# Rebuilding the middle part of a transformer kernel: loads, engines, order of tiles, and the hand-over to the last matrix products

## The chip, the cores and the metric

One core of one Trainium2 chip. The metric is the device time of one execution in microseconds (us); a version's time is the median of several executions, and a version is compared with the kernel before within one series of runs on one chip. The profile is one execution, recorded instruction by instruction.

In profile lines PE is TensorE (PEld its weight loads), DVE is VectorE, ACT is ScalarE, POOL is GpSimd; SPq and ACTq are the DMA queues of SyncE and ScalarE; L411 is a line of that run's own kernel. A timeline line gives start, duration, engine, line, what was done and how often, and in brackets the engine's idle time before it and what ended that. A line of waits gives who waited for whom, the total in us, the number of waits and the longest. "..." stands for lines left out. A "product" is one matmul instruction.

## The reference, cut to what matters

A recurrent attention over 64 segments (part A) gives `a`. Then, on 2048 rows of 1024 columns:

```python
h  = x + A(layernorm(x), ...)                 # part A: 64 segments, one after the other
# B, applied to hn = layernorm(h):
h1 = gelu(layernorm(hn) @ w1)                 # 1024 x 1024
#   four column groups of h1 shifted by -1, +1, -2, +2 rows
x1 = hn + shifted(h1) @ w2                    # 1024 x 1024
h2 = gelu(layernorm(x1) @ w3) @ w4            # 1024 x 3584 x 1024
out = h + x1 + h2
```

I call what stands up to `x1` and its normalised transpose `zT` the middle part (w1, w2), and the products with w3 and w4 the last part.

## The kernel before

Rows come in 16 tiles of 128, four tiles to a block. The middle part works by whole blocks: stage 1 of block b+1 (four tiles of sums, two norms, transposes, then 64 products with w1), then stage 2 of block b (for each tile 16 products with w2, a norm, transposes).

```python
def ln_apply(dst, src, tag):
    mv = _ln_stats(nc, sm, src, D, tag)             # VectorE: two bn_stats, one bn_aggr
    r = _rstd(nc, sm, mv, eps_t, tag)               # GpSimd: add, pow on 128x1
    nc.vector.tensor_scalar(dst[:], src[:], mv[:, 0:1], r[:], op0=ALU.subtract, op1=ALU.mult)

with tc.tile_pool(name="b1w", bufs=1) as b1w, tc.tile_pool(name="b1", bufs=2) as b1, ...:
    nc.sync.dma_start(w1[:], ...); nc.sync.dma_start(w2[:], ...); nc.sync.dma_start(w3[:], ...)

    def stage1(b):
        for tl in range(TPB):
            nc.scalar.dma_start(xt[:], x2[...]);  nc.scalar.dma_start(at[:], a_d[...])
            nc.gpsimd.tensor_tensor(ht[:], xt[:], at[:], op=ALU.add)
            nc.scalar.dma_start(h_d[...], ht[:])
            ln_apply(hn, ht, "l1"); ln_apply(u, hn, "l2")
            # eight transposes of u into PSUM on TensorE
            nc.vector.tensor_copy(uT[:, :, tl * 128:(tl + 1) * 128], pt[:])
        # 64 products with w1, a gelu on ScalarE after every eight

    def stage2(b):
        for tl in range(TPB):
            # 2 x 8 products with w2, x1 = ps + hn on VectorE
            ln_apply(z, x1, "l3")
            # eight transposes of z into PSUM
            nc.vector.tensor_copy(zT[:, :, tl * 128:(tl + 1) * 128], pt[:])
        nc.scalar.dma_start(zT_d[b], zT[:])
    # ... (loop over blocks left out)

wb4 = ctx.enter_context(tc.tile_pool(name="wb4", bufs=1))
nc.sync.dma_start(w4[:], ...)                       # 7 MB
with tc.tile_pool(name="b2", bufs=2) as b2:
    for b in range(NB):
        zT = b2.tile([128, NC, BT], BF16, tag="zT2")
        nc.scalar.dma_start(zT[:], zT_d[b])
        # 28 x 8 products with w3 and gelu, 8 x 28 products with w4, sums, output (left out)
```

A pool is a range of on-chip memory. A pool that is opened over the place of a closed one waits, by default, for that whole pool; `reuse_waits="tile"` makes its tiles wait for just the tiles that lay there.

## Time and profile before

| | before |
|---|---|
| median time | 2928.3 us (13 runs, 2924.8 to 2935.5) |
| part A (to its last product) | 2274.6 us |
| to the first product with w1 ("head") | 50.5 us |
| first w1 product to first w3 product | 206.5 us |
| last part | 392.3 us |

The stages are read from the order of TensorE's instructions in time. The whole span in 40 slices (73 us each), with TensorE's busy tenths and its granted clock in tenths:

```profile
PE   1599999999999999999999999999999367699999
PEclk9999999999999999999999999999999688899999
```

The reader is to see that after the start a single stretch, slices 32 to 35, is not full: 257 us in which the array waits and, after its longer waits, starts again at a low clock.

### The profile page before, as it was taken

How to read it: one execution, taken by the hardware profiler on the slowest of the kernel's cores; microseconds unless marked ns; L12 is line 12 of the kernel's file. 1: busy time of each engine (PE TensorE's matmuls, PEld its weight loads, DVE VectorE, ACT ScalarE, POOL GpSimd, SP SyncE). 2: the span in 40 equal slices, each digit the busy share in tenths (PEclk: the TensorE clock that was granted, in tenths of full speed). 3: DMA queues.
4: the chain of work that ended last, by engine and by line, in shares of the span. 5: the costliest groups of instructions: out<-in, count | busy, mean ns of one | idle time of the engine just before them, and what ended most of it. 6: DMA issues, size and time to landing. Idle time of an engine off the chain costs nothing.

```text
span 2923.9 us, 69270 instructions
## 1 busy us (share of the span) xinstructions
PE 2629.8 (90%) x29824; PEld 1517.4 (52%) x29824; DVE 1015.7 (35%) x3043; ACT 739.5 (25%) x1506; POOL 286.4 (10%) x496
## 2 busy tenths in 40 slices
PE   1599999999999999999999999999999367699999
PEld 1365555655655655555656655555555133344444
DVE  3233333333343333343333343333443454300000
ACT  1122222322233322332222233222232011112211
POOL 4000000000000000000000000000000431110110
PEclk9999999999999999999999999999999688899999
DMA  9999999999999999999999999999999721511010
GB/s 355 332 352 338 330 324 334 340 333 340 328 325 332 338 336 341 327 330 335 337 338 330 331 335 338 331 339 323 332 333 325 286 91 43 210 47 39 30 44 15
DMA packets 254227, 816.15 MB, mean 279 GB/s; under 512 B 28120, under 2 KB 52696, under 8 KB 252896
## 3 DMA queue, kind: packets, MB, share of 16 engines
q1 hardware_dynamic: 232256, 761.36, 72.7%
q0 software_dynamic: 11296, 25.20, 2.7%
q10 hardware_dynamic: 10368, 25.17, 2.3%
q8 instruction: 233, 3.82, 0.5%
q14 instruction: 74, 0.61, 0.1%
HBM read 775.44 MB, written 36.18 MB: 278 GB/s over the span
## 4 chain that ended last, share of the span: by engine, by line
PE 80%; DMA 9%; DVE 4%; POOL 3%; issue 2%; ACT 1%; SPq 0%; ACTq 0%; POOLq 0%
PE ps L207 41%; PE Uacc L290 15%; PE ps L454 7%; PE ps L469 7%; PE pr L215 6%; DMA a_d<-usb 4%; DMA xt<-in_A_x_dram 2%; PE ps L411 2%; PE pv L274 1%; DVE st L28 1%; PE ps L239 1%; POOL ht L397 1%; DVE usb L297 1%; ACT usb L296 1%; DMA at<-a_d 1%
## 5 line engine op out<-in xcount | busy, mean ns | idle before, releaser
L207 PEld LDWEIGHTS <-hT 128*64 128x64 bf16 x12288 | 723.6, 110 | 504.9 <-issue 55.0
L207 PE MATMUL ps<-ringw,hT 128*64 128x512 bf16 x3840 | 795.6, 380 | 10.7 <-DMA ringw<-in_A_Wk_dram 5.2
L210 ACT CAST Tsb<-ps 128x512 bf16<-128x512 f32 x768 | 447.5, 585 | 1029.0 <-PE ps L207 772.3
L207 PE MATMUL ps<-wq,hT 128*64 128x512 bf16 x3072 | 488.4, 382 | 25.9 <-DVE hT L302 24.0
L207 PE MATMUL ps<-wv,hT 128*64 128x512 bf16 x3072 | 486.7, 380 | 0.7 <-ACT Tsb L210 0.7
L290 PE MATMUL Uacc<-wo,oT 128*40 128x512 bf16 x2560 | 345.6, 381 | 0.5 <-ACT oT L277 0.5
L207 PE MATMUL ps<-wk,hT 128*64 128x512 bf16 x2304 | 322.5, 380 | 0.0
L290 PEld LDWEIGHTS <-oT 128*40 128x40 bf16 x4096 | 218.2, 100 | 179.7 <-issue 8.6
L226 DVE COPY QT<-pr 128x320 bf16<-128x320 bf16 x256 | 83.1, 324 | 514.1 <-PE pr L215 512.1
L290 PE MATMUL Uacc<-ringw,oT 128*40 128x512 bf16 x1536 | 234.0, 380 | 5.4 <-DMA ringw<-in_A_Wo_dram 4.5
L454 PE MATMUL ps<-zT,w 128*128 128x512 bf16 x896 | 195.5, 381 | 17.6 <-DMA zT<-zT_d 17.6
L469 PE MATMUL ps<-w,h3T 128*128 128x512 bf16 x896 | 194.0, 379 | 0.0
L215 PEld LDWEIGHTS <-Tsb 128*64 128x64 bf16 x4096 | 153.7, 110 | 71.3 <-ACT Tsb L210 22.9
L215 PE MATMUL pr<-ident,Tsb 128*64 128x128 bf16 x4096 | 171.2, 220 | 17.3 <-ACT Tsb L210 16.9
L242 DVE SCALAR_TENSOR_TENSOR ps<-ps,maskb 128x160 f32<-128x160 f32 x256 | 85.0, 332 | 276.3 <-PE ps L239 274.3
L315 POOL COPY hT<-xt 128x256 bf16<-128x256 bf16 x64 | 25.6, 400 | 1535.2 <-PE ps L207 1532.7
L254 DVE TENSOR_TENSOR Pp<-ps,sm 64x160 bf16<-64x160 f32 x512 | 165.1, 322 | 16.7
L277 ACT CAST oT<-pv 128x320 bf16<-128x320 f32 x256 | 110.2, 430 | 224.6 <-PE pv L274 220.5
L471 DVE TENSOR_TENSOR ot<-ps,rs 128x512 bf16<-128x512 f32 x32 | 22.1, 691 | 383.9 <-PE ps L469 383.9
L454 PEld LDWEIGHTS <-w 128*128 128x128 bf16 x896 | 87.9, 98 | 124.4 <-DMA zT<-zT_d 17.8
L264 DVE COPY pt<-pr 128x512 bf16<-128x512 bf16 x256 | 107.2, 419 | 128.6 <-PE pr L215 128.5
L456 ACT ACTIVATE h3T<-ps 128x512 bf16<-128x512 f32 x112 | 66.9, 597 | 329.5 <-PE ps L454 329.5
(74 smaller groups left out, 1867.8 us busy)
## 6 DMA issues: line engine op xcount, KB each, us to landing
ringw<-wst_d SPq DMA_DIRECT2D x1323, 512.0 KB, 5.9
w<-in_B_w_dram SPq DMA_DIRECT2D x2, 7168.0 KB, 29.3
wst_d<-ringw SPq DMA_DIRECT2D x21, 512.0 KB, 4.1
wq<-in_A_Wq_dram SPq DMA_DIRECT2D x12, 512.0 KB, 11.1
wv<-in_A_Wv_dram SPq DMA_DIRECT2D x12, 512.0 KB, 12.0
wo<-in_A_Wo_dram SPq DMA_DIRECT2D x10, 512.0 KB, 13.2
wk<-in_A_Wk_dram SPq DMA_DIRECT2D x9, 512.0 KB, 10.9
xt<-in_A_x_dram POOLq DMA_DIRECT2D x16, 256.0 KB, 6.1
```

The lines of the kernel that those rows point to most:

```text
L207: nc.tensor.matmul(ps[64 * j:64 * j + 64, :], lhsT=hT[:, c, :], rhs=ws[j][:, c4, :], start=(c == 0), stop=(c == NC - 1), tile_position=(0, ...
L210: nc.scalar.copy(sb[:], ps[:])
L215: nc.tensor.transpose(dst[64 * eh:64 * eh + 64, :], src[:, 64 * eh:64 * eh + 64], ident[:], tile_position=(0, 64 * eh))
L226: nc.vector.tensor_copy(dst[:, :, 0:R].rearrange("p (j hh) r -> p hh j r", j=2), pr[:].rearrange("p hh (j r) -> p hh j r", j=2)[:, :, :, 0:R],
L242: nc.vector.scalar_tensor_tensor(sc[:], ps[:], scale, maskb[:, None, :].to_broadcast([128, 4, R]), op0=ALU.mult, op1=ALU.add)
L254: nc.vector.tensor_tensor(pp[64 * j:64 * j + 64, :, 64 * j:64 * j + R], ex[64 * j:64 * j + 64], sm[64 * j:64 * j + 64, :, None].to_broadca ...
L264: nc.vector.tensor_copy(pt[:], pr[:])
L277: nc.scalar.copy(o[:].rearrange("p (j hh) q -> p hh j q", j=2), pv[:])
L290: nc.tensor.matmul(U[64 * dr:64 * dr + R, :], lhsT=o[:, lh, :], rhs=w[:, h2, 512 * dr:512 * dr + 512], start=(first and h4 == 0), stop=(la ...
L454: nc.tensor.matmul(ps[:], lhsT=w3[:, c, fb * 128:(fb + 1) * 128], rhs=zT[:, c, :], start=(c == 0), stop=(c == NC - 1))
L456: nc.scalar.activation(h3T[:, fb, :], ps[:], ACTF.Gelu_apprx_tanh)
L469: nc.tensor.matmul(ps[:], lhsT=h3T[:, fb, tl * 128:(tl + 1) * 128], rhs=w4[:, fb, dr * 512:(dr + 1) * 512], start=(fb == 0), stop=(fb == N ...
```

## The change

Its intent: fill the middle part's gaps. Inputs are loaded ahead of the weights and w3 later; the normalisations and one copy go from VectorE to ScalarE, the sum from GpSimd to VectorE, the second norm's statistics are worked out from the first's; the blocks are interleaved tile by tile; the last part's buffers are split and wait per tile, w4 comes in quarters.

```diff
     def ln_apply(dst, src, tag):
         ...
-        nc.vector.tensor_scalar(dst[:], src[:], mv[:, 0:1], r[:], op0=ALU.subtract, op1=ALU.mult)
+        nb_ = sm.tile([128, 1], F32, tag=tag + "_nb")
+        nc.vector.scalar_tensor_tensor(nb_[:], mv[:, 0:1], -1.0, r[:], op0=ALU.mult, op1=ALU.mult)
+        nc.scalar.activation(dst[:], src[:], ACTF.Identity, bias=nb_[:], scale=r[:])
...
+    def load_xa(tt):                       # xt and at, four buffers each
+        nc.sync.dma_start(xt[:], x2[tt * 128:(tt + 1) * 128, :])
+        li = nc.sync.dma_start(at[:], a_d[tt * 128:(tt + 1) * 128, :])
+    for tt0 in range(4):
+        first_ld = load_xa(tt0)
+    with tc.issue_after(first_ld.ins):
         nc.sync.dma_start(w1[:], ...)
         nc.sync.dma_start(w2[:], ...)
-        nc.sync.dma_start(w3[:], ...)
...
+        nc.vector.tensor_tensor(ht[:], xt[:], at[:], op=ALU.add)      # was GpSimd
+        nc.gpsimd.dma_start(h_d[tt * 128:(tt + 1) * 128, :], ht[:])   # was ScalarE's queue
+        mv, r = ln_apply(hn, ht, "l1")
+        nc.gpsimd.tensor_tensor(r2[:], r[:], r[:], op=ALU.mult)
+        nc.gpsimd.tensor_scalar(r2[:], r2[:], mv[:, 1:2], LN_EPS, op0=ALU.mult, op1=ALU.add)
+        nc.gpsimd.tensor_tensor(r2[:], r2[:], eps_t[:], op=ALU.pow)
+        nc.scalar.activation(u[:], hn[:], ACTF.Identity, scale=r2[:])
...
-        for b in range(NB):
-            stage1(b)
-            if b > 0:
-                stage2(b - 1)
-        stage2(NB - 1)
+    for b in range(NB + 1):
+        for tl in range(TPB):
+            if b + 1 < NB:
+                s1_tile(b + 1, tl)
+            if b < NB:
+                m1_part(b, range(tl * npart, (tl + 1) * npart))
+            if b > 0:
+                m2_tile(b - 1, tl)         # copies zT with nc.scalar.copy
+    with tc.issue_after(last_ld[0].ins):
+        for q in range(4):                 # w3 in quarters, after the last input
+            nc.sync.dma_start(w3[...], w3v[...])
...
-    wb4 = ctx.enter_context(tc.tile_pool(name="wb4", bufs=1))
-    nc.sync.dma_start(w4[:], ...)
-    with tc.tile_pool(name="b2", bufs=2) as b2:
-            zT = b2.tile([128, NC, BT], BF16, tag="zT2")
-            nc.scalar.dma_start(zT[:], zT_d[b])
+    b2z = ctx.enter_context(tc.tile_pool(name="b2z", bufs=2, reuse_waits="tile"))
+    wb4 = ctx.enter_context(tc.tile_pool(name="wb4", bufs=1, reuse_waits="tile"))
+    for q in range(4):
+        nc.sync.dma_start(w4[...], w4v[...])
+    with tc.tile_pool(name="b2", bufs=2, reuse_waits="tile") as b2:
+            zT = b2z.tile([128, NC, BT], BF16, tag="zT2")
+            nc.sync.dma_start(zT[:], zT_d[b])
```

(Cut: shapes, buffer counts, the other stores moved from ScalarE's to GpSimd's queue, the last part's loads moved to the SP queue with one `rs` buffer instead of two.)

## The prediction

> **What bounds the kernel now.** I read the busy slices of the page first, then the table of stretches, then the waits of TensorE, then the chain of waits in order of time, and last the groups of instructions for durations. In the slices TensorE is at 9 tenths from the second slice to slice 31, drops for eight slices and is full again: the program is a long recurrent part, a middle part with gaps, and two large matrix products. The diff touches only what comes after the recurrence, so I cut the span at the last recurrent tail (2274.6 us), the first product with w1 (2325), the last transposes of z (2514) and the first product with w3 (2531.5).
>
> The table of stretches (length, busy time of TensorE, its weight loads, VectorE, ScalarE, GpSimd, then granted clock, DMA share, GB/s):
> ```profile
> 0.00:2274.60 2274.60, 2098.89 (x27264) 1271.80 (x27264) 861.71 (x2754) 652.24 (x1360) 163.00 (x334) 1.00 0.94 334
> 2274.60:2325.00 50.40, 4.12 (x32) 3.19 (x33) 21.74 (x46) 0.37 (x1) 21.95 (x27) 0.54 0.92 345
> 2325.00:2514.00 189.00, 138.47 (x736) 66.78 (x735) 109.44 (x213) 20.07 (x33) 50.17 (x88) 0.86 0.22 80
> 2514.00:2531.50 17.50, 0.00 (x0) 0.00 (x0) 0.66 (x1) 0.00 (x0) 2.23 (x4) 0.50 1.04 406
> 2531.50:2923.90 392.40, 388.38 (x1792) 175.60 (x1792) 22.12 (x32) 66.86 (x112) 49.04 (x44) 1.00 0.13 45
> ```
> The first and last rows are full of matrix work at full clock. The three between are 257 us, in which TensorE is busy 143 us, part of it at a low clock (0.54, 0.86, 0.50). ScalarE is nearly empty there (20 us), VectorE has 132 us. That is the only place where the change can win.
>
> Who makes TensorE wait in 2274.6 to 2531.6:
> ```profile
> PE pt L406 <- DVE u L372: 68.2, 11, 22.4
> PE pt L433 <- DVE z L372: 24.1, 16, 5.7
> PE ps L454 <- DMA zT<-zT_d: 17.6, 1, 17.6
> PE ps L411 <- DVE uT L407: 4.4, 4, 1.9
> ```
> It waits for normalised tiles (u, z) from VectorE, 92 us, and once for a reload of zT. The chain of waits just before that reload and the last rows of it:
> ```profile
> 2512.70 0.56 DVE z L372
> 2513.31 0.64 PE pt L433 x8
> 2513.97 0.70 DVE zT L434
> 2514.69 7.78 DMA zT_d<-zT
> 2522.56 8.94 DMA zT<-zT_d
> 2531.55 8.51 PE ps L454 x32
> ```
> The reload is of block 0, written long before; it stands behind the store of block 3 because the new pool waits for the whole old pool, and both transfers run beside the 7 MB load of w4. Pure waiting, 17.6 us.
>
> The head, in order of time:
> ```profile
> 2276.76 0.67 ACTq L395 DMA_DIRECT2D at<-a_d  x1
> 2284.29 2.11 POOL L397 TENSOR_TENSOR ht<-xt,at 128x1024 bf16<-128x1024 bf16 x1 [7.52 <-DMA w<-in_B_w_dram]
> ...
> 2309.77 2.12 POOL L397 TENSOR_TENSOR ht<-xt,at 128x1024 bf16<-128x1024 bf16 x1 [7.86 <-DMA at<-a_d]
> ...
> 2325.06 16.23 PE L411 MATMUL ps<-uT,w 128*128 128x512 bf16 x64 [1.94 <-DVE uT L407]
> ```
> The first tile's input waits behind w1 and w2; w3 (7 MB, issued at 2293) then delays the next tiles, and the first add on GpSimd takes 2.11 us. Four tiles need 50 us.
>
> Durations used below, from the groups of the same stretch:
> ```profile
> L397 POOL TENSOR_TENSOR ht<-xt,at 128x1024 bf16<-128x1024 bf16 x16 | 33.9, 2117 | 76.7 <-DVE hn L372 53.3 <-DMA at<-a_d 15.9 <-DMA w<-in_B_w_dram 7.5
> L37 POOL TENSOR_TENSOR r<-r,eps_t 128x1 f32<-128x1 f32 x48 | 27.7, 580 | 3.2
> L28 DVE BATCH_NORM_STATS2 st<-x 128x6 f32<-128x512 bf16 x32 | 21.9, 685 | 0.4
> L427 DVE TENSOR_TENSOR x<-ps,hn 128x512 bf16<-128x512 f32 x32 | 21.7, 678 | 52.8 <-PE ps L425 52.7
> L413 ACT ACTIVATE h1T<-ps 128x512 bf16<-128x512 f32 x32 | 18.8, 597 | 125.8 <-PE ps L411 121.9 <-POOL r L37 3.5 <-issue 0.4
> ```
>
> **What the Trainium skill says.** (1) "TensorE: Matmul & The Clock Gate", "Wait — 56ns, not 53.3ns?": 512 columns take 215.7 ns warm and 426.7 cold, and part 1 that some 3.4 us of idling brings the cold state. The trace agrees: eight products per gelu, gelus 1.727 us apart, 0.216 each; and after each long gap weight loads 0.43 us apart and a granted clock of 0.5. (2) "ScalarE: Activation LUTs", "What ACT_TABLE_LOAD costs" and "Table sets": 186 ns plus 0.833 per element, about 93 more for each per-partition pointer, and copy and identity lie in every table set. The trace has 1012 ns for a 1024-element copy (186 + 853 = 1039) and 597 for a 512-element gelu (613), and one table load of 1.28 us in this part; no run has identity beside gelu yet. (3) "VectorE: DVE Perf Modes", the perf-mode tier table: a two-input add of bf16 in SBUF runs at 2 elements a cycle; my estimate from that page's formula is (512 + 151)/0.96 = 0.69 us for 1024. The trace has no such instruction. (4) "DMA: Bandwidth & Descriptors", "Queues, rings and completion order": issuing queues share the same 16 engines, each engine round-robins between them and takes each queue in ring order. The 7.5 us wait of the first tile, on another queue than w1 and w2, agrees.
>
> **The change, part by part.**
>
> VectorE per tile, before: six bn_stats 4.05, three aggregations 0.6, three normalisations 1.74 (0.54 + 0.65 + 0.55), two transposed copies 1.36, two adds from PSUM 1.36: 9.1 us, times 16 = 146. After: the statistics of hn are gone (the second norm's variance is worked out from the first's), and the normalisations and one copy go to ScalarE; added are the sum 0.69 and two one-element products, about 0.19 each as an aggregation (0.20): 4 x 0.68 + 2 x 0.2 + 0.38 + 0.69 + 0.68 + 1.36 = 6.2 us.
> ScalarE per tile, after: hn and z about 186 + 853 + 2 x 93 = 1.22 each, u 1.13, zT copy 1.01, two gelus 1.2: 5.8 us, less about 0.09 of overlap each, 5.2 to 5.8.
> GpSimd per tile: out goes the 2.12 us add and one of three rstd pairs (0.22 + 0.58); in come about 1.0 for r2 and two store issues of about 0.57: 2.12 + 2.4 = 4.5 before, about 3.8 after.
> TensorE per tile: 32 products x 0.216 = 6.9, two times eight transposes about 0.45 warm: 7.8. So TensorE becomes the bound of this part, if the order lets it.
>
> The head: inputs of four tiles (2 MB) go ahead of w1 and w2, w3 comes only after the last input. Landing at about +3.5 us (a late, undisturbed input took 2.9 to 3.0), then VectorE 3.0 us per tile (0.69 + 1.36 + 0.2 + 0.19 + 0.68) for four tiles, 12, and the last tile's latency (rstd 1.1, hn 1.2, u 1.1, transposes 1.0 cold, copy 0.7) about 5: 20 us instead of 50.4. **Saves 30.**
> The body is interleaved tile by tile. First block, w1 products alone: four tiles of 16 x 0.216 + 0.45 + 0.6 for waits = 4.5, plus 1.7 for the cold start: 20. Twelve full tiles at 7.8 + 0.5 for waits: 100. Last block, w2 products alone: now every tile took 4.52 us (z transposes at 2486.45 and 2490.97); z is 0.65 slower on ScalarE and has one small step more, but zT leaves VectorE's loop: 4.7 x 4 = 19. Sum 139 instead of 189. **Saves 50.**
> The transition: waits per tile instead of per pool, with zT's buffers where w1 lay and w3 long there. zT of block 0 can arrive during the last block, so the w3 products follow at once; the z transposes of the last tile slip in among them. w4 (7 MB, 33.6 us to landing) must wait for h1T, but has 224 x 0.216 = 48 us before its first use. **Saves 17.5**, and the cold start of 1.7 is not paid again.
> The last 392 us: the loads on another queue, one rs buffer instead of two. The sum (2.11 us) must follow the previous tile's last eviction (0.69) and has 28 x 0.216 = 6 us until it is needed: 0.
>
> Sum: 2927 - 30 - 50 - 17.5 - 1.7 = 2828 us.
>
> **Rivals.** A: *the zT reload queues behind w4.* Both are now on one queue, w4 first in the program. If the order in the queue is the program's, zT waits for the last use of h1T and then shares with 7 MB: some 20 to 25 us of stall, 2850. Against it: zT is ready to issue an iteration earlier and the order follows readiness. I give it one in four.
> B: *a new chain.* With z on ScalarE, behind gelus and other copies in strict order, and a fixed order on TensorE, tiles could take 10 us instead of 8.3: 12 x 1.7 = +20, 2848. For it: VectorE was already at only 109 of 189 us, so latency and not load made the waits. Against it: stage 1 now runs a whole block ahead, so u is ready long before.
> C: *table switches.* If identity needed its own set, each tile would pay at least four switches of 1.28, 82 us or more, ScalarE at 11 us per tile becomes the bound, and the gain shrinks to some 50 us: 2875. The skill's table sets speak against it.
> D: *the head is bound by bandwidth*: 4 MB before w1 is whole, at 345 GB/s 12 us; below 20, so hidden.
>
> **Range and chances.** Time **2828 us**; A and B each cost some 20, both together give the upper end, a smooth order with tiles at 7.8 and a head of 16 us the lower: **2806 to 2858**. Faster by over 2% means below 2868.5, 58 of the 99 us expected; the head and the transition alone give 47. Chances: faster 0.94, within 2% 0.05, slower 0.01.
>
> **What would show it.** The first w1 product about 20 us after the last tail; the first w3 product about 159 us after it, with no wait for zT; VectorE about 100 us and ScalarE about 90 in that stretch; one table load; a granted clock near 1 from the first block on; the last stretch still 390 to 392. Wrong would be: tiles over 10 us with TensorE waiting for ScalarE; a gap of 20 us before the w3 products; a changed recurrent part; a stop of TensorE at the first w4 product.

## The result, and the profile after

The changed kernel took 2839.9 us (8 runs, 2835.8 to 2844.8) against 2928.3 us. The ratio is 0.9698, 95% interval 0.9688 to 0.9707. A ratio here is the mean time of one kernel's fast runs over that of the other's fast runs of the same rounds, so it is not quite the ratio of the medians quoted.

The table of stretches of the changed kernel, cut at part A's last product, the first w1 product, the start of the second block, the end of its last full tile, and the first w3 product (columns as in the prediction):

```profile
0.00:2276.90 2276.90, 2100.98 (x27264) 1272.65 (x27264) 861.37 (x2754) 651.92 (x1360) 163.01 (x334) 1.00 0.93 333
2276.90:2301.40 24.50, 4.17 (x34) 3.19 (x33) 11.75 (x25) 10.77 (x10) 10.96 (x26) 0.58 0.95 345
2301.40:2323.20 21.80, 17.98 (x97) 8.23 (x97) 15.30 (x34) 15.21 (x18) 13.42 (x31) 0.92 0.69 240
2323.20:2424.20 101.00, 95.03 (x539) 44.69 (x539) 55.13 (x109) 52.44 (x61) 33.31 (x76) 1.00 0.45 169
2424.20:2446.90 22.70, 16.80 (x104) 8.21 (x103) 13.73 (x28) 10.25 (x9) 7.63 (x16) 0.95 0.47 168
2446.90:2839.90 393.00, 389.27 (x1794) 175.84 (x1792) 22.12 (x32) 67.88 (x113) 34.56 (x17) 0.99 0.16 57
```

From the end of part A to the first w3 product it was 257 us and is 170. Its main row, 101 us, has TensorE busy 95 at full clock. VectorE fell from 132 to 96 us in this part, ScalarE rose from 20 to 89. The last part did not gain. Who makes TensorE wait in the middle part now:

```profile
PE pt L430 <- ACT u L427: 21.3, 4, 12.7
PE pt L461 <- ACT z L374: 11.9, 16, 4.3
PE ps L438 <- DVE uT L431: 2.8, 2, 2.0
```

92 us of waiting for normalised tiles became 33, of which 19.5 are the head's two waits (12.69 and 6.85). The 17.6 us wait for zT has no line any more. What is left is in four places. The timeline of the changed kernel shows each: in the head (2287), at the first block's end (2323), once in every tile (2343 and 2352), and at the end of the middle part (2446):

```profile
2287.50 0.69 DVE L417 TENSOR_TENSOR ht<-xt,at 128x1024 bf16<-128x1024 bf16 x1 [0.24 <-DMA h_d<-ht]
...
2323.18 1.67 PE L438 MATMUL ps<-uT,w 128*128 128x512 bf16 x7 [2.00 <-DVE uT L431]
...
2343.55 0.62 PE L461 MATMUL pt<-ident,z 128*128 128x128 bf16 x8 [0.53 <-ACT z L374]
...
2352.22 0.62 PE L461 MATMUL pt<-ident,z 128*128 128x128 bf16 x8 [0.53 <-ACT z L374]
...
2446.07 1.03 PE L461 MATMUL pt<-ident,z 128*128 128x128 bf16 x8 [4.25 <-ACT z L374]
2446.89 23.44 PE L497 MATMUL ps<-zT,w 128*128 128x512 bf16 x97
```

The two steady tiles give the period: 2352.22 - 2343.55 = 8.67 us.

One caution for all comparisons below: part A, which no edit touches, ended between 2270 and 2279 us in the profiles, a scatter larger than the smallest effects. I therefore give for each run both its time and, from its profile, the three stages after part A (head; first w1 to first w3 product; last part). Before: 50.5, 206.5, 392.3, together 649.3 us. Changed: 24.5, 145.5, 393.0, together 563.0 us.

### The profile page after: what moved, and what is told of

Same layout as the page of the kernel before. It is cut to its first block, busy times and chain, and to the rows that moved or that the text cites. A ratio compares the mean times of both kernels' runs of the same rounds, so it can differ in the third digit from the quotient of the medians.

```text
span 2839.9 us, 69387 instructions
## 1 busy us (share of the span) xinstructions
PE 2624.2 (92%) x29824; PEld 1512.8 (53%) x29824; DVE 979.4 (34%) x2979; ACT 808.5 (28%) x1570; POOL 262.9 (9%) x500
## 4 chain that ended last, share of the span: by engine, by line
PE 82%; DMA 9%; DVE 3%; ACT 2%; issue 2%; POOL 1%; SPq 0%; ACTq 0%; POOLq 0%; DVEq 0%
PE ps L207 42%; PE Uacc L290 14%; PE ps L497 7%; PE ps L512 7%; PE pr L215 6%; DMA a_d<-usb 4%; DMA xt<-in_A_x_dram 2%; PE ps L453 2%; DMA ringw<-wst_d 2%; PE pv L274 1%; PE ps L239 1%; DVE usb L297 1%; ACT usb L296 1%; DVE st L28 1%; ACT z L374 1%
```

## The experiments

Twelve kernels ran; all gave correct results. The kernel before took 2925.7 us in the first series (e1 to e4), 2924.9 in the second (e6, e7, e8, e10) and 2929.8 in the third (e5, e11, e12, e13), which ran on another chip than the first two. Runs of different series, the changed kernel's own among them, are therefore compared by their ratios to the kernel before and by stages. The edits are cut to the lines that matter, and some are put in words.

### Each part alone

**e1_transition.** The kernel before with only the hand-over changed:

```diff
+    b2z = ...tile_pool(name="b2z", bufs=2, reuse_waits="tile")
-    wb4, b2: default waits; w4 in one load; zT from pool b2, loaded from ScalarE's queue
+    wb4, b2: reuse_waits="tile"; w4 in quarters; zT from pool b2z, loaded from SP's queue
```

> The kernel before with the transition alone changed: zT, w4 and the second part's pools wait per tile, w4 in quarters, zT loaded from the SP queue. My theory: the 17.6 us wait for zT before the first w3 product vanishes, all else as before: 2928 - 17.5 = 2910 us. The changed kernel showed no gain beyond that there (its last stretch was 393.0 us against 392.4), so no extra cold start is expected to be saved. Rival A (zT queues behind w4 on SP): w4's first quarters must wait for h1T, zT lands late, 2920 us or no gain.

Measured: 2908.6 us, ratio 0.9943 (0.9927 to 0.9960), 17.0 us faster by the medians. Stages 50.3, 191.2, 392.4. The amount is as expected and the last part shows no further gain. Rival A did not come: zT went out at 2481.88, w4 at 2509.39. Which of the edit's four pieces did it, this run can't tell.

**e2_head.** The kernel before with only the loads changed:

```diff
-        w1, w2, w3 first on SP; xt, at from ScalarE's queue, two buffers
+        xt, at of four tiles first on SP, four buffers; then w1, w2; w3 after the last input
```

> The kernel before with the input loads alone changed: inputs of four tiles on the SP queue ahead of w1 and w2, four buffers, w3 after the last input. Work stays on its engines. My theory: the head (last recurrent tail to first w1 product) falls from 50 us to about 30: 3.5 landing, add 2.1, VectorE 5 us a tile for four tiles, 4 latency; body unchanged: 2908 us. Rival: the head is bound by VectorE's and GpSimd's chain and not by the transfers: about 45 us stay, 2923 us. Second rival: inputs are also late in the body, so the body gains too: below 2900.

Measured: 2917.9 us, ratio 0.9973 (0.9958 to 0.9988), 7.8 us faster, so a miss between my theory and its rival. Stages 36.8, 212.3, 393.5. The head fell by 13.7 us, not 20, and the body gave back 5.8: some of it where TensorE, at the first block's end, waits 5.6 us for u instead of 3.3, as VectorE still has its 9 us of work a tile. Late inputs were a part of the head's time; the old work was the rest.

**e3_offload.** The kernel before with only the engines changed (old order, queues and pools; one `rs` buffer so that it fits):

```diff
-        tensor_scalar, sum on GpSimd, statistics of hn, zT copy on VectorE
+        activation(Identity) on ScalarE, sum on VectorE, r2 from r and mv, zT copy on ScalarE
```

> The kernel before with the engines alone changed: normalisations and the zT copy on ScalarE, the add on VectorE, the second norm's scale worked out from the first; order of blocks, queues and pools as before. My theory: VectorE falls from 9 to 6 us a tile, but the fixed order by blocks leaves TensorE waiting between blocks: a part of the body's gain, some 20 us of 43, plus some 5 in the head: about 2900 us. Rival (load is all, order does not matter): the whole 43 us of the body, 2880 or below. Rival (latency is all): ScalarE's slower steps make the chain longer, 2925 or slower.

Measured: 2901.6 us, ratio 0.9915 (0.9901 to 0.9930), 24.1 us faster, as the theory said. Stages 48.4, 182.6, 392.2. Lighter engines help, but the order by blocks keeps TensorE waiting.

### Each part left out

**e4_old_engines.** The changed kernel with the old engines (the reverse of the edit above, in the interleaved order).

> The changed kernel with the old engines: normalisations with full statistics and the zT copy on VectorE, the add on GpSimd; interleaving, loads and transition as changed. My theory: VectorE's 9.1 us a tile (about 8.5 when issued back to back) now exceeds TensorE's 7.8, so tiles take 9 to 9.5 instead of 8.66 and the head is 8 to 10 us longer: 2840 + 8 + 10 = 2858 us. Rival (order is all): 2840 to 2845. Rival (load is all): the body goes back to 189 us, 2880.

Measured: 2873.6 us, ratio 0.9822 (0.9807 to 0.9837), 33.8 us slower than the changed kernel's 2839.9. My 2858 was too low. Stages 37.1, 168.1, 391.6: 12.6 us of it in the head, 22.6 in the body. Two steady tiles of this run on TensorE:

```profile
2357.56 0.62 PE L454 MATMUL pt<-ident,z 128*128 128x128 bf16 x8 [1.93 <-DVE z L372]
...
2359.23 0.62 PE L423 MATMUL pt<-ident,u 128*128 128x128 bf16 x8 [0.40 <-DVE u L372]
...
2368.03 0.62 PE L454 MATMUL pt<-ident,z 128*128 128x128 bf16 x8 [1.93 <-DVE z L372]
```

The period is 10.47 us, more than VectorE's 9.1 us of load. I had sized this run by load, but in such a period no engine is full: TensorE is busy for 8.15 us, VectorE for 8.03, GpSimd for 5.78. The waits for z and u are 1.40 and 0.40 us longer than the changed kernel's 0.53 and none, which is all of the 1.80 us between 8.67 and 10.47. In the chain to z, the statistics of x1 are done at 2364.46, but GpSimd has begun its 2.11 us sum of a later tile at 2364.43 and takes up z's scale only at 2366.53. So the trace puts the period down to the chain of one tile through VectorE and GpSimd; no run tests that by itself. The same edit is worth 24.1 us in the old order and 33.8 in the new one.

**e10_blocks.** Everything but the interleaving: the edits of the first three runs together, in the old order of blocks.

> Everything of the change but the interleaving: loads first, work on the new engines, transition per tile, in the old order of blocks (stage 1 of block b+1 whole, then stage 2 of block b). Theory A (the parts add): 2926 - 17 - 8 - 24 = 2877 us, and the interleaving is worth the rest, some 37 us. Theory B (the engines and the loads do all, interleaving little): 2850 or below. Theory C (they overlap, gains are less than their sum): 2885 or above.

Measured: 2870.3 us, ratio 0.9812 (0.9792 to 0.9832), 54.5 us faster than before; the three parts alone sum to 48.9. So the times add, within the interval (some 6 us either way), but not stage by stage: alone the three take 16.0 us off the head and 33.4 off the body, together 28.3 and 26.7. That the totals agree is two opposite differences that cancel. What is left to the changed kernel is about 30 us. It is the interleaving's with one reservation: this run also keeps the stores on ScalarE's queue and the last part's loads on GpSimd's, which was not run apart. Stages 22.2, 179.8, 392.2: the head is even shorter than in the changed kernel, and the whole difference is in the body. Of its 34 us, TensorE is idle for 24 more; the other 10 are the same work at a lower granted clock (140.2 us busy at 0.85, against 129.8 at 0.98). TensorE's waits of this run:

```profile
PE pt L425 <- ACT u L422: 21.8, 6, 12.2
PE pt L452 <- ACT z L374: 19.4, 10, 4.7
PE ps L430 <- DVE uT L426: 14.5, 4, 9.6
```

The 9.6 us, for example, come at the start of a block, where no other block's products are in line behind. A store has a part in them: just before, VectorE's sum for the last tile waits 5.18 us for the store of an earlier sum (two buffers, as in the head), which runs beside the load of w3; four such stores landed after 8.9 us in the median.

**e5_pool_waits.** The changed kernel with the per-tile waits taken back:

```diff
-    b2z, wb4, b2: reuse_waits="tile"
+    b2z, wb4, b2: default (wait for the whole pool)
```

> The changed kernel with the transition's waits set back: the second part's pools wait for the whole first part's pools, all else as changed. Theory: zT of block 0 and w4 wait for the last store of zT, and w4's four quarters stand before zT in the same queue; 17 to 25 us of wait before the first w3 product: 2857 to 2865 us. Rival (the queue change and the early w3 hid the reload, the tile waits do nothing): 2840.

Measured: 2840.6 us, ratio 0.9694 (0.9681 to 0.9707): the same as the changed kernel. My theory fell; the rival was right. The timeline of the SP queue and of TensorE in this run:

```profile
2443.65 0.81 SPq L492 DMA_DIRECT2D zT<-zT_d  x2
2454.97 9.31 SPq L488 DMA_DIRECT2D w<-in_B_w_dram  x4
```

```profile
2447.78 1.03 PE L461 MATMUL pt<-ident,z 128*128 128x128 bf16 x8 [4.25 <-ACT z L374]
2448.71 50.44 PE L497 MATMUL ps<-zT,w 128*128 128x512 bf16 x224
```

The waits did change: in the changed kernel zT goes out at 2419.24 and w4 at 2441.96, here 24 and 13 us later. But zT still goes out ahead of w4, because its pool now lies over w1, whose pool is free with the last w2 product, and not behind w4's place over the buffers that hold the last zT until it is stored. The queue's own waits say so: zT's load waits for the last products with w2 here (`SPq L492 <- PE ps L453: 95.1, 1, 95.1`) and for products with w1 in the changed kernel (`SPq L492 <- PE ps L438: 50.8, 1, 50.8`), and w4's here for the last store (`SPq L488 <- DMA zT_d<-zT: 10.1, 1, 10.1`). Its load then fits into the 4.25 us for which TensorE waits for the last z anyway. And w4, even 13 us later, has the 48 us of the w3 products. So in the changed order the new place of zT's buffer and its turn in the queue are enough, and the waits per tile add nothing; that this also holds for the 17 us of e1_transition is not shown, as that place alone, with whole-pool waits in the old order, was not run.

### The four places of what is left

**e6_ht_inplace.** In the head, the third tile's sum waits for the store of the first one's sum, as both share two buffers. Here the sum is written into x's buffer:

```diff
-        ht = b1.tile([128, D], BF16, tag="ht", bufs=2)
+        ht = xt                                            # xt: 6 buffers instead of 4
```

> The changed kernel with the sum of x and a written into x's buffer (six of them instead of four, the two of the sum dropped), so that the third and fourth tile of the head need not wait for the stores of the first and second. Theory: the head falls from 24.5 to about 20.5 us as I had predicted it: 2836 us. Rival: the wait goes over to the inputs, which come late beside w1 and w2, or is given back at the first block's end: within 1 us of the changed kernel, 2839 to 2841.

Measured: 2843.5 us, ratio 0.9719 (0.9703 to 0.9736). No gain, as the rival said, and perhaps a loss. Stages 22.5, 154.2, 393.2: the head is 1.9 us shorter, the body 8.7 longer. In the head the third sum starts 5.48 us after the first and the fourth 8.60, where the changed kernel has 7.13 and 11.05 (the 0.24 us in its line above is only the end of that delay). Two lines of this run:

```profile
2297.00 0.69 DVE L417 TENSOR_TENSOR xt<-xt,at 128x1024 bf16<-128x1024 bf16 x1 [2.18 <-DMA at<-a_d]
...
2337.63 0.74 PE L461 MATMUL pt<-ident,z 128*128 128x128 bf16 x8 [3.33 <-ACT z L374]
```

VectorE now waits for the fifth tile's input, which is behind w1 and w2; and, as I read it, the fixed order of instructions came out worse at the start of the second block (3.33 us there, where the changed kernel has 0.53).

**e11_w2_late.** The changed kernel with w2, which is needed a block later than w1, behind the inputs of tiles 4 to 7:

```diff
-        nc.sync.dma_start(w2[:], ...)                      # right behind w1
+    for tt0 in range(TPB, 2 * TPB):
+        last4 = load_xa(tt0)
+    with tc.issue_after(last4.ins):
+        nc.sync.dma_start(w2[:], ...)
```

> The changed kernel with the load of w2 put behind the inputs of tiles 4 to 7. Theory: what holds the first block and the start of the second is the late inputs of tiles 4 to 7 (7.9 us on the queue behind w1 and w2); they come some 6 us earlier, the waits of 0.7, 1.0 and 2.0 us there vanish: 2835 to 2837 us. Rival: VectorE's and ScalarE's chain for tiles 4 to 7 is the bound: 2839 to 2841.

Measured: 2833.2 us, ratio 0.9669 (0.9656 to 0.9682), an interval that lies below that of the changed kernel; the gain is somewhat larger than I had expected. Stages 24.1, 141.1, 391.7. From the first w1 to the first w2 product it takes 21.2 us instead of 25.7, and the waits of 0.7, 1.0 and 2.0 us at the first block's end are gone. So late inputs held that place, and not the chain of ScalarE and VectorE.

**e7_late_z.** The changed kernel with the z transposes moved from behind the first to behind the eighth of the next tile's w2 products:

```diff
         for dr in range(2):
             # eight products with w2, x1 = ps + hn
+            if dr == 0 and zq:
+                z_tr(*zq.pop())                            # transposes of the tile before
```

> The changed kernel with the eight transposes of z put in the middle of the next tile's w2 products (after eight of sixteen) instead of after the first one. Theory: the wait of 0.53 to 0.59 us in each of some twelve tiles vanishes, 6 to 7 us: 2833 us, tiles at about 8.1 us. Rival: ScalarE's or VectorE's chain is the true period and the wait moves to another place: 2838 to 2841.

Measured: 2832.0 us, ratio 0.9684 (0.9667 to 0.9702), which overlaps the changed kernel's interval, so by time alone it is unclear. The stages are 23.9, 143.7, 392.5, 1.8 us less in the body. Two things make this so little:

```profile
2319.95 3.14 PE L438 MATMUL ps<-uT,w 128*128 128x512 bf16 x7 [2.00 <-DVE uT L431]
...
2352.46 0.62 PE L430 MATMUL pt<-ident,u 128*128 128x128 bf16 x8 [0.49 <-ACT u L427]
...
2353.35 0.61 PE L468 MATMUL pt<-ident,z 128*128 128x128 bf16 x8
...
2360.92 0.62 PE L430 MATMUL pt<-ident,u 128*128 128x128 bf16 x8 [0.49 <-ACT u L427]
```

The wait for z is gone, and one of 0.49 us for u has come in its place: the eight tiles with stage 1 take 8.46 us instead of 8.67. The four full tiles without stage 1 have lost the wait altogether: 7.35 us instead of 8.11. Together that is 4.7 us, of 6 to 7 expected. The rest was given back where the edit changes nothing: in the first block, after the same waits (0.70, 1.01 and 2.00 us), seven products took 3.14 us here and 1.67 in the changed kernel. From the first w1 to the first w2 product it took 28.7 us at a granted clock of 0.81, against 25.7 at 0.93; from there to the first w3 product 114.9 us against 119.8, which is the edit's 4.9. e5_pool_waits, with the changed kernel's order in this place, had 27.9 us at 0.85. So the clock in that block differs from profile to profile, which is worth 2 to 3 us, and the body's times below are split at the first w2 product. A half-confirmed theory: right in the tiles, except for the wait that moved to u.

**e8_late_z_pre.** The run before, and the first 24 products with w3 put ahead of the last tile's z transposes:

```diff
+    zT0 = b1.tile([128, NC, BT], BF16, tag="uT", name="zT0")
+    nc.sync.dma_start(zT0[:].rearrange("p c t -> p (c t)"), zT_d[0])
+    w3_pre()                                               # three groups of eight products
     z_tr(*zq.pop())
     b1ctx.close()
```

> The run before, and 24 products with w3 for the first block put ahead of the last tile's z transposes (zT of block 0 reloaded into a free buffer of uT). Theory: the wait of 4.25 us, the cold transposes (0.6) and the cold start of the w3 products (some 1.7) vanish: 6 to 7 us less than the run before, 2827 us. This is what I had predicted the transition to do. Rival: the products wait for w3 or zT or a free PSUM bank instead: no gain.

Measured: 2827.7 us, ratio 0.9666 (0.9648 to 0.9684). Stages 24.4, 137.9, 391.2: against the run before the body is 5.8 us shorter (5.3 of it after the first w2 product: 109.7 against 114.9) and the last part 1.3, although the last tile's transposes now fall into it. That is the 6 to 7 us expected; by time alone it is unclear, as the two intervals overlap. The end of the middle part in this run:

```profile
2436.35 0.81 PE L455 MATMUL ps<-w,h1T 128*128 128x512 bf16 x3
2437.00 5.34 PE L497 MATMUL ps<-zT,w 128*128 128x512 bf16 x24
2442.18 0.61 PE L468 MATMUL pt<-ident,z 128*128 128x128 bf16 x8
```

No idle time, and transposes at 0.61 us for eight instead of 1.03. This is the hand-over that the prediction had described.

### Together

**e12_late_z_pre_w2** has the edits of e8 and e11, **e13_best** those and e6's.

> Late z transposes, early w3 products and the late load of w2 together. Theory: the gains add, 2827.7 less 3 to 5: 2823 to 2825 us. Rival: 2828.

> The run before with the sum written into x's buffer as well (six x buffers). Alone that gained 2 us in the head and gave it back at the first block's end, where the inputs came late; with the inputs early the head's 2 us should stay: 2820 to 2823 us. Rival: it stays a loss of 2 to 4 us, by a worse fixed order at the start of the second block: 2826 to 2828.

Measured: 2827.7 us, ratio 0.9647 (0.9632 to 0.9662), and 2826.0 us, ratio 0.9643 (0.9628 to 0.9657). Both beat the changed kernel and the kernel before; their intervals and e8's (0.9648 to 0.9684) overlap, so the times don't rank the three. By stages e12 is 24.4, 131.4, 391.1, together 547.0 us, the shortest of all after part A (16.0 less than the changed kernel), and e13 is 22.5, 135.7, 391.2, together 549.4. e12's expected 2823 to 2825 was missed in the median, in a series in which the kernel before was 5 us slower than in e8's; by stages the two gains add (9.5 and 6.1 against 16.0). The split body says the same: e11 has 21.2 us to the first w2 product and 119.9 after it, e8 28.2 and 109.7, e12 21.7 and 109.7. e13's expected 2820 to 2823 was missed too, and its rival's 2826 to 2828 fits: for writing into x's buffer there is no gain to be shown here.

## Why the prediction was right or wrong

It said 2828 us and a range of 2806 to 2858; 2839.9 lies in it. The 88.4 us gained compare with 99 forecast. The misses don't cancel: against its stages the profile is 4.5 us longer in the head, 6.5 in the body and 2.3 in the last part. By its steps:

- **The bound and the place of the gain:** right. The slices were misread (the full ones begin with the third, and four are not full, not eight), and 146 us of VectorE work, added up from mean durations, is more than the 132 us busy that the same text reads off; nothing hung on either. Part A and the last part are within 2.3 and 0.7 us of before in the profiles, and TensorE is busy 95 of 101 us in the main row.
- **The head, 20 us:** measured 24.5. The term left out is the two-buffer sum that waits for a store: 1.9 us, by e6_ht_inplace. The other 2.6 us were not traced to one cause.
- **The first block, 20 us:** measured 21.8, with 3.7 us of waits at its end where 2.4 was allowed for all four tiles. e11_w2_late showed late inputs as their cause.
- **Twelve full tiles, 100 us:** measured 101, with 0.52 to 0.59 us of wait in each where I had put 0.5. The agreement is closer than the working: the eight tiles with both sets of transposes took 8.67 us, not 8.3, and the four of the last full block, which have no stage 1 and only one set, took 8.11. e4_old_engines (10.47 us a tile) and e10_blocks (about 30 us lost) show that both the engines and the order are needed.
- **The last block, 19 us:** measured 22.7. The step that failed is "the z transposes of the last tile slip in among" the w3 products. They did not; the fixed order put them ahead, and TensorE stood for 4.25 us. e8_late_z_pre showed what that cost.
- **The transition, 17.5 us:** right in amount (17.0 in e1_transition), but not for the reason given. "Waits per tile instead of per pool" are not what removes it in the changed kernel, as e5_pool_waits showed; the buffer's new place and turn are enough. So the amount was partly luck. The 1.7 us of the "cold start" that "is not paid again" failed: it was paid, as the clock was low after the 4.25 us wait (the transposes there took 1.03 us, not 0.62), and was won back only in e8_late_z_pre (1.3 us in the last part, in spite of some 0.45 us of transposes moved into it).
- **Rivals:** A, zT behind w4, did not come: zT went out 22.7 us ahead of w4. B, a new chain, came at a fraction of its size: 0.53 us of wait in each tile, and 8.67 us a tile at most, not 10. The prediction has A and B together as its upper end, 2858; their costs add up to some 2868. C, table switches: the middle part has one table load of 1.28 us, so none. D, the head bound by bandwidth, did not show as the bound of the first product, but at the first block's end, as said.
- **VectorE about 100 us and ScalarE about 90 in the stretch:** 96 and 89. The durations taken from the Trainium skill held. A normalisation with one per-partition pointer took 1134 ns and with two 1240, where my estimate by "ScalarE: Activation LUTs", "What ACT_TABLE_LOAD costs", is 1132 and 1225. Identity and gelu alternated with one table load of 1283 ns, as the same page's "Table sets" has it that identity is in every set. The bf16 sum of 1024 took 687 ns against the estimate of 0.69 us from "VectorE: DVE Perf Modes", the perf-mode tier table.

What stays open: whether the same place of zT's buffer would do in the old order with whole-pool waits, how much of e10's 30 us belongs to the queue of the stores, and whether e13 differs from e12.

## What to carry to other kernels

When one engine should be full and is not, interleave the next stage's preparation with this stage's products as well as taking work off the other engines: here the same lighter engines were worth 24 us in the old order and 34 in the new one. A gap costs more than its idle time, as the products after it run at a low clock (10 of the 34 us that e10_blocks lost in the body). Load what is needed first ahead of large weights, and count the inputs of the second block too. At a hand-over between two phases, look at which buffer lies over which and at who is first in the queue, and put a few of the next phase's products ahead of the last slow chain; a version that looks complete still had 16 us of such places.

## What the Trainium skill lacked or had wrong

- "TensorE: Matmul & The Clock Gate", "Part 4: PE-mode transpose", says that the fast state doesn't engage for transposes. Here eight transposes among products took 0.61 to 0.62 us and after a wait of 4.25 us 1.03: in these runs they ran at the state that the products before them had left. Whether transposes alone would bring that state, no run shows.
- "DMA: Bandwidth & Descriptors", "Anatomy of one DMA": my estimate by its fit is about 2.6 us for the 256 KB of a store from GpSimd's queue. With w1 and w2 in flight the first store of the head, issued at 2281.60, freed its buffer at 2287.5, 5.9 us later; the page has no figure for a transfer that shares the engines with a large load.
- No page says how buffers placed over one another decide who waits for whom. In e1_transition the place, the waits and the queue of one reload were worth 17.0 us; in the changed order the waits alone were worth nothing (e5_pool_waits, 2840.6 us against 2839.9).
